# Issuing the 32 loads of weight halves from SP in place of ACT in a fused attention and feed-forward kernel

## The chip, the cores and the metric

The kernel runs on one core of a Trainium2 chip. The metric is the device time of one execution in microseconds (us), as the median of several runs. A profile is one further execution, recorded by the hardware profiler: TensorE (PE, with its weight loads PEld), VectorE (DVE), ScalarE (ACT), GpSimd (POOL) and SyncE (SP), and the 16 DMA engines that move data between the chip's memory (HBM) and the on-chip buffers. SP and ACT both issue DMAs; such an issue is shown as SPq or ACTq.

## The reference, cut to what matters

Windowed attention with a few always visible "sink" keys, followed by a feed-forward block with a softplus between its two products:

```python
scores = scale * np.matmul(q, k.transpose(0, 1, 3, 2))      # q, k, v: 4 x 8 heads x 768 x 64
keep = is_sink | in_window                                   # 4 sinks, window of 128
a = softmax(np.where(keep, scores, -1e9))
x = (a @ v).transpose(0, 2, 1, 3).reshape(3072, 512)
h = x @ w_in                                                 # 512 x 2048
out = (np.maximum(h, 0.0) + np.log1p(np.exp(-np.abs(h)))) @ w_out
```

The two weight matrices arrive as 64-bit floats, 16.8 MB together.

## The kernel before, in words

The 3072 rows are cut into 12 chunks of 256. Each chunk goes through the attention of its 8 heads, then through 8 blocks of the feed-forward part. The program is a software pipeline over heads: while chunk n is in the feed-forward part, chunk n+1 is in attention.

The weights are read once. `_weight_dma` (line 358) loads one half block of 512 KB in raw form: `wi` is the first matrix, `wo` the second, the first digit is the block, the second the half, and an `r` at the end marks the raw words (`wi20r`). There are 32 such loads, each into a buffer of its own, so none waits for a buffer. After the load a half is turned into two 32-bit parts in four stages: a cast of the upper words into a scratch tile `upper` (stage a, on DVE, ACT or POOL), a shift-and-or into a word tile (stage c, line 403, always DVE), a rounded high part (d) and the rest (l). Stage a is the first reader of the raw words.

The first 17 head steps are written out by hand in the string `START` (letters are parts of the pipeline, numbers are heads); after that a steady loop runs. In `START` the letter `w` loads the next weight half, `L8`, `L10`, ... load the keys and queries of a pair of heads, `S7` computes the scores of head 7, `T7` its softmax, and `a c d l` take the next half through the four stages. Heads 0 to 7 belong to chunk 0, heads 8 to 15 to chunk 1. In the names of tiles the chunk comes first: `k1_2`, `q1_2` are keys and queries for heads 2 and 3 of chunk 1.

PE and SP issue their instructions in the order in which the program is written. ACT, DVE and POOL get an order that a scheduler worked out at build time. Each engine then goes through its order strictly: an instruction whose inputs are not there holds up all behind it on that engine.

Two kinds of waits matter for a DMA. First, buffers: keys of pairs from head 6 on share two buffers (`tag="qkh"`), so `k1_2` can be loaded only when PE has finished `S7`, the last reader of `k0_6`; likewise `k1_4` waits for `S9`, and `qk2_1` for `S15`. Second, semaphores: the built program gives eight completion semaphores to the DMAs of SP and ACT in turn, and a DMA is issued only after the last one that used its semaphore has landed. So about eight are in flight at a time.

Of the kernel before, what the change touches and what calls it, by code (L numbers as in the profile page):

```python
# [14 lines left out]
I16 = mybir.dt.int16  # L15
# [18 lines left out]
WH = WC // 2  # L34
# [323 lines left out]
def _weight_dma(c, s, k, half):  # L358

    src = c.a["w"][s, k, :, half * WH : (half + 1) * WH]
    tag = f"{WTAG[k]}{s}{half}"
    r = c.wp.tile([P, 4 * WH if c.w64 else 2 * WH], I16 if c.w64 else F32, tag=tag, name=f"{tag}r")
    if c.w64:
        c.nc.scalar.dma_start(r[:, : 4 * WH - 1], src.bitcast(I16)[:, 1:])
    else:
        c.nc.scalar.dma_start(r[:, :WH], src)  # L370
    c.raw[s, k, half] = r


# [136 lines left out]
def _fast(c):  # L510
# [23 lines left out]
    def dma(i):  # L534
        if dmas:
            _weight_dma(c, *dmas.pop(0))
# [135 lines left out]
def _general_weights(c):  # L672

    nc = c.nc
    for e in ((s, k, half) for s in range(FP) for k in range(2) for half in range(2)):
        _weight_dma(c, *e)
        r = c.raw[e]
        t = c.stg.tile([P, WH], I32, tag="stg", name="gt%d_%d_%d" % e)
        if c.w64:
            mid, top16 = _weight_words(r)  # L680
            top = c.gp.tile([P, WH], I32, tag="g_top", name="gtop%d_%d_%d" % e)
            u = c.gp.tile([P, WH], I32, tag="g_u", name="gu%d_%d_%d" % e)
            nc.vector.tensor_copy(top[:], top16.bitcast(I16))
            nc.vector.tensor_scalar(u[:], top[:], 4, 0x7FF, ALU.logical_shift_right, ALU.bitwise_and)
            nc.vector.tensor_scalar(u[:], u[:], -896.0, 0.0, ALU.add, ALU.max)
            nc.vector.tensor_scalar(u[:], u[:], 255.0, None, ALU.min)
            nc.vector.tensor_scalar(t[:], top[:], 19, 0x00780000, ALU.logical_shift_left, ALU.bitwise_and)
            nc.vector.scalar_tensor_tensor(t[:], u[:], 23, t[:], ALU.logical_shift_left, ALU.bitwise_or)
            nc.vector.scalar_tensor_tensor(t[:], top[:], -0x80000000, t[:], ALU.bitwise_and, ALU.bitwise_or)
            nc.vector.scalar_tensor_tensor(t[:], mid, 13, t[:], ALU.logical_shift_right, ALU.bitwise_or)  # L690
        else:
            nc.vector.tensor_copy(t[:].bitcast(F32), r[:, :WH])
        c.word[e] = t
        _weight_high(c, e, "A")
        _weight_low(c, e, "V")
# [208 lines left out]
```

## Time and profile before

| what | value |
|---|---|
| time, median of 3 runs | 738.54 us (738.09 to 738.70) |
| the profiled execution: its own time, its span | 735.03 us, 733.3 us |
| PE busy in the span | 699.0 us (95%) |
| DVE, ACT, POOL busy | 567.5 us (77%), 448.7 us (61%), 429.0 us (59%) |
| bytes moved by DMA | 63.21 MB, 16.77 MB of it on ACT's queue |
| size of a load: weight half, k, q, vr of chunk 0, qk of one head | 511.8, 200, 256, 128, 2 x 164 KB (KB of 1024 bytes) |

Shares are averages over the whole span. The page's 40 slices show that the first seventh is another stage than the rest: there DMA and DVE digits are high and PE's digits are not yet all nines; after it PE stands at 9 until the last slice. The change touches only loads that are issued in this first part, so the rows below come from there.

### The profile page before, as it was taken

The numbers are of one execution on the slowest core, as the hardware profiler recorded it, in microseconds if no ns is written. First come the engines' busy times: TensorE is split into PE (matmuls) and PEld (weight loads), VectorE is DVE, ScalarE is ACT, GpSimd is POOL, SyncE is SP. The second block draws the span as 40 slices with busy tenths as digits, with TensorE's granted clock in tenths as the row PEclk, the third lists the DMA queues.
The fourth block names the chain that finished last, engine by engine and source line by source line (L and its number), as shares of the span: only waits on it lengthen the run. The fifth ranks groups of instructions, "written<-read, shape, count | busy, mean of one in ns | idle before, by whom it ended". The sixth has DMA issues, their size and how long they took to land.

```text
span 733.3 us, 13867 instructions
## 1 busy us (share of the span) xinstructions
PE 699.0 (95%) x4489; PEld 621.4 (85%) x4489; DVE 567.5 (77%) x1608; ACT 448.7 (61%) x1098; POOL 429.0 (59%) x773
## 2 busy tenths in 40 slices
PE   4788899999999999999999999999999999999996
PEld 3567688988999999888898999998898998998995
DVE  5899997887887887887987988888887887754331
ACT  3577865765666666765666765765666666644331
POOL 4866476675655765775765665666666576563110
PEclk9899999999999999999999999999999999999998
DMA  8877611411321321312222222221222222100001
GB/s 299 298 261 227 196 40 48 119 53 44 100 67 48 106 67 49 103 55 60 74 74 67 77 77 67 77 75 46 71 66 78 77 67 77 60 11 1 29 1 35
DMA packets 40876, 63.21 MB, mean 86 GB/s; under 512 B 4635, under 2 KB 22363, under 8 KB 40795
## 3 DMA queue, kind: packets, MB, share of 16 engines
q1 hardware_dynamic: 36042, 45.47, 21.4%
q10 hardware_dynamic: 4752, 16.77, 6.7%
q8 instruction: 38, 0.62, 0.4%
q14 instruction: 44, 0.35, 0.2%
HBM read 55.93 MB, written 6.29 MB: 85 GB/s over the span
## 4 chain that ended last, share of the span: by engine, by line
PE 80%; DVE 7%; ACT 5%; POOL 5%; issue 2%; DMA 1%; ACTq 0%; SPq 0%; POOLq 0%; DVEq 0%
PE h L459 33%; PE acc L496 10%; PE acc L498 10%; PE acc L497 10%; PE x L333 6%; PE t L297 2%; PE s L230 2%; PE s L231 2%; ACT a L250 2%; PE x L327 2%; PE s L227 1%; DVE wt L403 1%; ACT mt L467 1%; ACT mt L468 1%; POOL vs L159 1%
## 5 line engine op out<-in xcount | busy, mean ns | idle before, releaser
L459 PE MATMUL h<-xh,wi 128*128 128x256 f32 x1536 | 254.1, 288 | 0.0
L459 PEld LDWEIGHTS h<-xh,wi 128*128 128x128 f32 x1536 | 211.7, 192 | 1.3 <-issue 0.3
L52 POOL TENSOR_SCALAR gh<-mt 128x512 fp32r<-128x512 f32 x91 | 56.6, 622 | 169.4 <-DVE mt L474 164.3
L459 PE MATMUL h<-xl,wi 128*128 128x256 f32 x768 | 154.7, 283 | 0.0
L496 PE MATMUL acc<-wo,gh 128*128 128x512 f32 x384 | 152.3, 397 | 0.0
L498 PE MATMUL acc<-wo,gl 128*128 128x512 f32 x384 | 151.3, 394 | 0.8 <-DVE gl L56 0.8
L497 PE MATMUL acc<-wo,gh 128*128 128x512 f32 x384 | 151.1, 393 | 0.0
L474 DVE SCALAR_TENSOR_TENSOR mt<-h,mt 128x512 f32<-128x512 f32 x96 | 66.1, 689 | 73.0 <-ACT mt L468 63.9
L466 ACT ACTIVATE mt<-h 128x512 f32<-128x512 f32 x96 | 57.1, 595 | 102.6 <-PE h L459 102.1
L459 PEld LDWEIGHTS h<-xl,wi 128*128 128x128 f32 x768 | 119.8, 192 | 0.0
L250 ACT ACTIVATE a<-a,stats 128x136 f32<-128x136 f32 x192 | 76.1, 397 | 59.7 <-DVE stats L249 59.7
L264 POOL TENSOR_SCALAR a<-a,rc 128x128 f32<-128x128 f32 x180 | 68.1, 390 | 43.0 <-ACT mt L466 28.3
L498 PEld LDWEIGHTS acc<-wo,gl 128*128 128x128 f32 x384 | 72.4, 189 | 17.7 <-DVE gl L56 1.2
L496 PEld LDWEIGHTS acc<-wo,gh 128*128 128x128 f32 x384 | 72.4, 189 | 13.0 <-issue 0.5
L56 DVE TENSOR_TENSOR gl<-mt,gh 128x512 fp32r<-128x512 f32 x96 | 77.4, 806 | 4.1 <-POOL gh L52 4.0
L497 PEld LDWEIGHTS acc<-wo,gh 128*128 128x128 f32 x384 | 72.5, 189 | 8.9
L308 POOL TENSOR_SCALAR_AFFINE_SELECT pt<-tl 128x256 fp32r<-128x256 f32 x80 | 57.9, 724 | 17.6 <-DVE tl L56 17.6
L467 ACT ACTIVATE mt<-mt 128x512 f32<-128x512 f32 x96 | 60.8, 633 | 3.1
L468 ACT ACTIVATE mt<-mt 128x512 f32<-128x512 f32 x96 | 60.7, 632 | 3.1
L48 ACT CAST qkh<-qk 128x656 fp32r<-128x656 f32 x80 | 59.5, 744 | 2.4 <-DMA qk<-qk 2.3
L308 POOL TENSOR_SCALAR_AFFINE_SELECT pt<-th 128x256 fp32r<-128x256 f32 (+1 forms) x96 | 41.8, 435 | 27.5 <-ACT th L48 20.2
L56 DVE TENSOR_TENSOR kl<-qk,qkh 128x400 fp32r<-128x400 f32 x80 | 53.7, 671 | 2.5
(183 smaller groups left out, 1247.2 us busy)
## 6 DMA issues: line engine op xcount, KB each, us to landing
qk<-qk SPq DMA_DIRECT2D x160, 164.0 KB, 3.0
vr<-v SPq DMA_DIRECT2D x32, 192.0 KB, 2.8
out<-o SPq DMA_DIRECT2D x24, 256.0 KB, 2.3
q<-q SPq DMA_DIRECT2D x8, 256.0 KB, 4.9
vr<-v SPq DMA_DIRECT2D x16, 128.0 KB, 2.2
k<-k SPq DMA_DIRECT2D x8, 200.0 KB, 4.8
wi00r<-w ACTq DMA_DIRECT2D x1, 511.8 KB
wi01r<-w ACTq DMA_DIRECT2D x1, 511.8 KB
```

The lines of the kernel that those rows point to most:

```text
L48: nc.scalar.copy(out, in_)
L56: (nc.vector if eng == "V" else nc.gpsimd).tensor_tensor(out, a, b, ALU.subtract)
L250: nc.scalar.activation(a, a, AF.Exp, bias=nm, scale=-1.0, accum_out=sm[:, j : j + 1])
L264: (nc.vector if eng == "V" else nc.gpsimd).tensor_scalar(a, a, rc[:, j : j + 1], 0.0, ALU.mult, ALU.add)
L308: nc.gpsimd.affine_select(pt[:, e, :, 1], src[:], [[0, CH], [1, P]], ALU.is_ge, 0.0, base=0, channel_multiplier=-1)
L459: nc.tensor.matmul(h[:, j], wt, x, start=k == 0, stop=k >= len(prods) - 2, skip_group_check=True)
L467: nc.scalar.activation(t[:], t[:], AF.Exp, scale=-1.0)
L468: nc.scalar.activation(t[:], t[:], AF.Ln, bias=1.0)
L474: nc.vector.scalar_tensor_tensor(t[:], h[:], 0.0, t[:], ALU.max, ALU.add)
L496: nc.tensor.matmul(acc[:], gh[:, j, q], wh, start=f == 0, stop=False, skip_group_check=True)
L497: nc.tensor.matmul(acc[:], gh[:, j, q], wl, start=False, stop=False, skip_group_check=True)
L498: nc.tensor.matmul(acc[:], gl[:, j, q], wh, start=False, stop=f == 2 * FP - 1, skip_group_check=True)
```

## The change

`_weight_dma` is called by the letter `w` of `START` and, in the fallback path, by `_general_weights`. Its DMA is now issued by SP (`nc.sync`) where it was issued by ACT (`nc.scalar`). Nothing else is edited; the fallback path isn't entered with these inputs.

```diff
@@ _weight_dma
     if c.w64:
-        c.nc.scalar.dma_start(r[:, : 4 * WH - 1], src.bitcast(I16)[:, 1:])
+        c.nc.sync.dma_start(r[:, : 4 * WH - 1], src.bitcast(I16)[:, 1:])
     else:
-        c.nc.scalar.dma_start(r[:, :WH], src)
+        c.nc.sync.dma_start(r[:, :WH], src)
```

SP before, the stretch between the last loads of chunk 0 and those of chunk 1 (`k1_0`: chunk 1, heads 0 and 1; the last number of a name is only a count):

```order
L201 DMA vr0_2_176<-v 128x2x128
L174 DMA k1_0_210<-k0 128x400
L176 DMA q1_0_212<-q0 128x512
L174 DMA k1_2_249<-k0 128x400
L176 DMA q1_2_251<-q0 128x512
L201 DMA vr0_3_391<-v 128x2x128
L174 DMA k1_4_485<-k0 128x400
```

SP now, from the same `k1_0` on:

```order
L174 DMA k1_0_210<-k0 128x400
L176 DMA q1_0_212<-q0 128x512
L368 DMA wi11r_214<-w 128x2047
L368 DMA wo00r_216<-w 128x2047
L174 DMA k1_2_249<-k0 128x400
L176 DMA q1_2_251<-q0 128x512
L368 DMA wo01r_253<-w 128x2047
L368 DMA wi20r_275<-w 128x2047
L368 DMA wi21r_312<-w 128x2047
L368 DMA wo10r_314<-w 128x2047
L368 DMA wo11r_334<-w 128x2047
L368 DMA wi30r_367<-w 128x2047
```

Six weight loads now stand behind `k1_2`, which waits for `S7`. On ACT the same stretch, as a difference (minus is before, plus would be now):

```order
 L250 ACTIVATE a_0_178,sm_2_234<-a_0_178,stats 128x136 x2
 L48 COPY th_0_244<-t_0_241 128x256
-L368 DMA wo01r<-w 128x2047
 L250 ACTIVATE a_0_178,sm_3_263<-a_0_178,stats 128x136 x2
 L262 ACTIVATE a_0_178<-a_0_178,rc_0_179 128x128 x2
-L368 DMA wi20r<-w 128x2047
 L250 ACTIVATE a_1_277,sm_4_279<-a_1_277,stats 128x136 x2
 L48 CAST upper_167<-wi01r 128x512
```

ACT loses its issues and keeps the order of the rest. The orders of DVE, POOL and PE in this path are the same in both programs.

## Rows read from the trace of the kernel before

**Rows 1.** Stages: busy us of each engine (instructions), PE clock, DMA share, GB/s

```profile
20.00:40.00 20.00, 15.89 (x75) 10.19 (x73) 18.85 (x67) 10.86 (x40) 17.04 (x26) 0.95 0.87 286
...
80.00:100.00 20.00, 17.72 (x118) 14.87 (x118) 19.64 (x48) 13.98 (x32) 8.20 (x14) 1.00 0.39 98
100.00:120.00 20.00, 20.00 (x125) 16.94 (x123) 16.03 (x43) 11.84 (x29) 14.04 (x25) 1.00 0.16 45
80.00:85.00 5.00, 3.47 (x29) 3.24 (x29) 4.93 (x10) 4.02 (x9) 2.32 (x4) 1.00 0.88 209
```

**Rows 2.** Chain that ended last, 8 to 50 us: start, us, engine, tile, line

```profile
12.68 0.09 ACTq L368
...
29.79 0.47 DVE upper L50
30.25 0.38 DVE s L243 x2
...
48.03 0.09 ACTq L368
```

**Rows 3.** Timeline of SP's issues, 24 to 33 us: start, us, line, out<-in

```profile
24.95 0.33 SPq L174 DMA_DIRECT2D k<-k  x1
25.32 0.60 SPq L176 DMA_DIRECT2D q<-q  x1
25.96 0.43 SPq L201 DMA_DIRECT2D vr<-v  x1
32.15 0.33 SPq L174 DMA_DIRECT2D k<-k  x1
```

**Rows 4.** Timeline of PE, scores of pairs of heads: S7, S9, S12

```profile
23.86 1.06 PE L227 MATMUL s<-k,q 128*128 128x264 f32 x4
...
30.99 1.13 PE L227 MATMUL s<-k,q 128*128 128x264 f32 x4 [1.11 <-DVE stats L249]
...
45.38 1.05 PE L227 MATMUL s<-k,q 128*128 128x264 f32 x4
```

**Rows 5.** Timeline of ACT's issues: two weight halves

```profile
12.44 0.33 ACTq L368 DMA_DIRECT2D wo01r<-w  x1
16.35 0.33 ACTq L368 DMA_DIRECT2D wi20r<-w  x1
```

**Rows 6.** Timeline of DVE, 28.9 to 34 us: start, us, line, out<-in

```profile
28.96 0.16 DVE L256 TENSOR_SCALAR sm<-sm 128x2 f32<-128x2 f32 x1
...
29.24 0.44 DVE L50 CAST upper<-wo01r 128x512 f16<-128x512 bf16 x1
...
29.70 0.55 DVE L50 CAST upper<-wi20r 128x512 f16<-128x512 bf16 x1
...
30.98 0.73 DVE L403 SCALAR_TENSOR_TENSOR wt<-wo01r,upper 128x512 int32<-128x512 int32 x1
...
32.40 0.98 DVE L256 TENSOR_SCALAR sm<-sm 128x2 f32<-128x2 f32 x1
...
33.49 1.71 DVE L403 SCALAR_TENSOR_TENSOR wt<-wi20r,upper 128x512 int32<-128x512 int32 x1
```

**Rows 7.** DMA issues: engine, count, KB each, us from issue to landing

```profile
wi30r<-w ACTq DMA_DIRECT2D x1, 511.8 KB, 6.3
...
wi51r<-w ACTq DMA_DIRECT2D x1, 511.8 KB, 5.1
...
wo50r<-w ACTq DMA_DIRECT2D x1, 511.8 KB, 10.2
```

**Rows 8.** Timeline, 75 to 84 us: the load of qk2_1, the cast of wi70

```profile
75.06 1.11 SPq L181 DMA_DIRECT2D qk<-qk  x2
...
83.07 0.77 ACT L48 CAST upper<-wi70r 128x512 f16<-128x512 bf16 x1
```

**Rows 9.** Timeline of POOL, 32 to 35 us: low parts of weight halves

```profile
32.09 1.26 POOL L56 TENSOR_TENSOR wi<-wt,wi 128x512 fp32r<-128x512 f32 x1
33.39 1.27 POOL L56 TENSOR_TENSOR wo<-wt,wo 128x512 fp32r<-128x512 f32 x1
```

## The prediction, made before the changed kernel had run

> **What bounds the kernel now.** I read the busy shares first, then stages of 20 us, then the chain of waits in the stage where the loads lie, then the timelines of SP, PE and DVE there, and last the list of DMA issues. Over the whole span PE is the busiest engine, and in the stage from 100 to 120 us it is busy all 20.00 us [rows 1]. But the 32 loads are issued before that, and there another engine sets the pace: DVE is busy 18.85 us of 20 in the stage from 20 us and 19.64 us in the one from 80 us, the first and the last of four such stages, while PE has 15.89 and 17.72 [rows 1]. The reader is to see in the chain that around 30 us it runs on DVE from one instruction to the next: the cast of a weight half into `upper`, then the softmax of scores [rows 2]. So a stop of DVE at 30 us has no cover: what stands behind it feeds ACT, POOL and PE, and PE is full after 100 us and has no room to win time back. DMA engines are busy 0.87 of the stage from 20 us and move 286 GB/s, so a full stretch carries 286 / 0.87 = 329 GB/s, or 321 KB per us [rows 1].
>
> **The change part by part.** *ACT loses 32 issues.* One takes 0.33 us or somewhat more of ACT's sequencer [rows 5], at least 32 x 0.33 = 10.6 us in all. ACT does arithmetic for 10.86 us of 20 in the stage from 20 us [rows 1], so most of it lies beside idle time. On the chain, issues of line 368 appear as five pieces of about 0.09 us, the first at 12.68 and the last at 48.03 us [rows 2]: 5 x 0.09 = 0.45 us to gain. The bounds are 0 (ACT only waits a little longer for DVE) and 10.6 us (every issue on the path); I take 0.45, since the chain shows the pieces themselves.
>
> *SP gains the 32 issues, in the order in which the program is written.* The first five halves stand ahead of `k1_2` in SP's order. Before, SP came to `k1_2` early and stood at it: it was issued at 24.95 us [rows 3], and S7, whose four matmuls release its buffer, started at 23.86 and ended 1.06 us later, at 24.92 [rows 4]. The wait has been harmless, because only loads of keys, queries and values stood behind it. Now six weight halves stand there. Of these ACT issued `wo01` at 12.44 and `wi20` at 16.35 us [rows 5], some 13 and 10 us ahead of the point at which SP can pass S7. Nothing in the change moves S7: its inputs are loaded before the first half, and up to 24 us DVE, POOL and ACT read only halves that stay ahead of the wait.
>
> *When the two halves come.* SP issues `k1_2` at 24.95, `q1_2` at 25.32, and the third load, now `wo01`, at 25.96; the one after that follows 0.43 us later [rows 3], so `wi20` at 26.4 us. The nearest row for its landing is `wi30`, which before was issued beside the same `k1_2` and `q1_2` and took 6.3 us [rows 7]: `wi20` lands at 26.4 + 6.3 = 32.7 us. Before, DVE cast `wo01` at 29.24 and `wi20` at 29.70 us [rows 6]. DVE will stop at the first and again at the second, and the second ends it: 32.7 - 29.70 = 3.0 us late. From below: the four loads are 200 + 256 + 512 + 512 = 1480 KB, 4.6 us at the full rate, which from 24.95 ends at 29.6 us if issue and landing cost nothing at all, that is no stop. The shortest landing of a half, 5.1 us [rows 7], gives 31.5 us and a stop of 1.8 us. From above: the longest landing, 10.2 us in a deep queue [rows 7], gives 36.6 and 6.9 us. I take 3.0: the queue behind k and q is that of `wi30`.
>
> *What stands behind the stop.* On DVE the softmax of the next head, whose end released PE for S9 in the chain; S9 began at 30.99 us after a wait of 1.11 us for DVE [rows 4]. S9 in turn releases `k1_4`, issued at 32.15 us [rows 3], so the next gate on SP moves with DVE. Then the DMA queue is full and the consumers have moved 3 us back as well. The tightest of the following loads is `q1_4`, read by S12 at 45.38 us [rows 4]. From `k1_2` to `q1_4` the new order has 200 + 256 KB, six halves, 128 KB of `vr0_3`, three halves, and 200 + 256 KB: 456 + 3072 + 128 + 1536 + 456 = 5648 KB, 17.6 us at 321 KB per us. With 6.3 - 4.6 = 1.7 us for issue and landing, it is there at 24.95 + 1.7 + 17.6 = 44.3 us; S12 will ask at about 45.38 + 2.6 = 48.0 us. It costs nothing, with 3.7 us of cover.
>
> *The last halves.* `wi70` to `wo71` now stand behind `qk2_1`, which waits for S15: 75.06 us before [rows 8], 77.6 now. SP issues two transfers and then `wi70`, about 78.8; with 6.3 us it lands at 85.1, and ACT casts it at 83.07 + 2.6 = 85.7 us [rows 8]. This is covered by 0.6 us, and the later halves are read later still.
>
> *Sum.* +3.0 - 0.45 = +2.55 us on the profiled execution: 735.03 + 2.55 = 737.6 us. Its span is 733.3 us, and the 1.7 us around it do not change. The median of the runs, 738.54 us, stands 3.5 us above the profiled execution; the same addition gives 741.1 us.
>
> **A rule that speaks against this.** The stage from 20 us shows the 16 DMA engines 0.87 busy whichever of the two engines issues [rows 1], and the change moves no byte more. The Trainium skill, "DMA: Bandwidth & Descriptors", section "Issuing engines are not separate DMA queues", says that DMAs from different issuers share the same 16 engines and that issuing from several only saves the sequencer's issue time, usually small beside the transfer. By that rule alone the sum would be the 0.45 us on ACT and no more; it becomes rival A. The trace agrees that an issue is short, 0.33 us [rows 5], but it also shows SP standing at a buffer's wait until 24.95 us [rows 3], which the rule does not speak of.
>
> **The rivals.** *A, the place of the issue does not matter.* The halves come in time after all, because SP's gate opens earlier or the data of the first 25 us runs ahead. For it: half the loads before the gate are in the same order as before. Against it: even at the full rate without any latency the second half would be there at 29.6 us, a tenth of a microsecond before its use. Time: 738.54 - 0.45 = 738.1 us.
>
> *B, the stop is paid back on DVE.* Not slower: in 32 to 35 us POOL works on low parts of halves, 1.26 and 1.27 us [rows 9], and DVE's rows beside them are long: `sm` takes 0.98 us where one at 28.96 took 0.16, the shift-and-or 1.71 where the one before took 0.73 [rows 6]. If DVE's stop lets POOL get through before DVE reaches these, 0.82 + 0.98 = 1.8 us return. It decides when the stop is no longer than these 1.8 us, the shorter of the bounds above: 738.54 + 1.8 - 1.8 - 0.45 = 738.1 us. Against it: POOL's second row works on a half that ACT rounds behind DVE's softmax, so it moves with DVE and meets it again.
>
> *C, a second stop at S12.* The slowest busy stretch, from 80 to 85 us, carried 209 GB/s at 0.88, 238 GB/s or 232 KB per us [rows 1]. At that rate `q1_4` is there at 24.95 + 1.7 + 24.3 = 51.0 us, 3.0 after S12 asks: 744.1 us. For it: one queue now holds the keys behind nine halves. Against it: the stage in question has run at 329.
>
> *D, faster.* ACT's issues cost more than the chain shows, since a wait for a semaphore stops ACT too. If a third of the 10.6 us lay on the path and the halves came in time, 738.54 - 3.5 = 735.0 us. Against it: DVE, not ACT, is full in these stages [rows 1].
>
> **How the numbers follow.** A measurement of this kernel can tell about 0.2% from no change, 1.5 us. The forecast, one stop of DVE for about 3 us, has 0.52, with 739.8 to 742.6 us as its own range; 0.03 of it lies within 1.5 us. A has 0.15, B 0.08, C 0.13, D 0.12. Slower is 0.52 - 0.03 + 0.13 = 0.62, the same 0.15 + 0.08 + 0.03 = 0.26, faster 0.12. The range leaves out most of D and the top of C and of the upper bound: 737.8 to 744.3 us.
>
> **What would show it.** Right: SP's `k1_2` still issued near 25 us with the weight halves right behind; idle time on DVE before the casts of `wo01` and `wi20` near 30 us, put down to their DMAs, 3 us together; a dip of the DMA rate between 20 and 26 us; PE's later work the same and shifted by 2 to 3 us. Wrong: no wait on DVE for a weight half (A), DVE's `sm` and shift-and-or near 33 us short (B), PE waiting for q at S12 (C), or ACT's chain shorter by microseconds (D). The forecast fails altogether if S7 ends much earlier than 24.9 us, or if the loads before the gate are slower in one queue than in two, so that a half ahead of it comes late.

## The result, and the profile after

The changed kernel takes 740.87 us (median of 6 runs, 739.32 to 742.90), the kernel before, run beside it, 738.12 us (6 runs): a ratio of 1.0048, 95% interval 1.0032 to 1.0065, so 2.4 to 4.8 us slower. The profiled execution took 739.32 us with a span of 737.6 us, 4.3 us more than that of before; the rows below explain these two executions, while the medians lie 2.75 us apart. The engines' busy times changed little (PE 699.5 us, DVE 564.5, ACT 448.7, POOL 427.8; DVE has 3.0 us less than before), so the time lies in waits.

SP first: the timeline of its issues from 25 to 36 us (start, us, engine queue, line, operation, tile), to be laid beside [rows 3].

```profile
25.56 0.33 SPq L174 DMA_DIRECT2D k<-k  x1
25.94 0.43 SPq L176 DMA_DIRECT2D q<-q  x1
26.41 0.43 SPq L368 DMA_DIRECT2D wo01r<-w  x1
26.89 0.43 SPq L368 DMA_DIRECT2D wi20r<-w  x1
...
29.85 1.01 SPq L368 DMA_DIRECT2D wi30r<-w  x1
30.90 0.62 SPq L201 DMA_DIRECT2D vr<-v  x1
31.56 0.52 SPq L368 DMA_DIRECT2D wi31r<-w  x1
33.72 0.33 SPq L368 DMA_DIRECT2D wo20r<-w  x1
35.22 0.33 SPq L368 DMA_DIRECT2D wo21r<-w  x1
```

`k1_2` is still let through by S7, 0.6 us later than before, and the six halves follow at once. The timeline of DVE from 29.7 us shows what that does; the bracket at a row's end is the idle time before it and what ended it. It answers to [rows 6].

```profile
29.76 0.17 DVE L257 RECIPROCAL rc<-sm 128x2 f32<-128x2 f32 x1
33.73 0.46 DVE L50 CAST upper<-wo01r 128x512 f16<-128x512 bf16 x1 [3.80 <-DMA wo01r<-w]
34.08 0.21 DVE L269 TENSOR_TENSOR sa<-a,rc 128x64 f32<-128x64 f32 x1
35.23 0.46 DVE L50 CAST upper<-wi20r 128x512 f16<-128x512 bf16 x1 [0.94 <-DMA wi20r<-w]
...
37.83 0.16 DVE L256 TENSOR_SCALAR sm<-sm 128x2 f32<-128x2 f32 x1
38.02 0.17 DVE L257 RECIPROCAL rc<-sm 128x2 f32<-128x2 f32 x1
38.10 0.67 DVE L403 SCALAR_TENSOR_TENSOR wt<-wi20r,upper 128x512 int32<-128x512 int32 x1
...
41.85 0.74 DVE L243 COPY_PREDICATED s<-diag,s 128x128 f32<-128x128 int32 x2 [1.90 <-PE s L227]
```

DVE stands for 3.80 us before the cast of `wo01` and for 0.94 us before that of `wi20`: 4.74 us in all, where before it had no wait for a weight half. `wo01` comes into use 33.73 - 26.41 = 7.3 us after its issue and `wi20` 8.3 us. The second is now a link of the chain that ended last (start, us, what), where before the chain around 30 us went from one DVE instruction to the next [rows 2]:

```profile
26.89 8.32 DMA wi20r<-w
```

The SP rows tell the same from another side. Eight loads can be in flight, so the eleventh from `k1_2` on, `wo20`, waits for the third to land: it goes out at 33.72, as DVE's cast of `wo01` begins. The twelfth goes out at 35.22, as the cast of `wi20` begins.

The same stretches as windows (start:end; length, then busy us and count of PE, PEld, DVE, ACT and POOL; granted PE clock; DMA share; GB/s), to be read against [rows 1]:

```profile
20.00:26.00 6.00, 5.75 (x26) 3.72 (x25) 5.16 (x19) 3.02 (x13) 4.51 (x6) 0.76 0.00 0
26.00:32.00 6.00, 3.83 (x18) 2.44 (x18) 3.64 (x16) 2.52 (x9) 5.78 (x13) 1.00 0.73 219
32.00:34.00 2.00, 0.00 (x0) 0.00 (x0) 0.27 (x1) 0.00 (x0) 1.03 (x1) 0.79 1.02 334
34.00:36.00 2.00, 0.00 (x0) 0.00 (x0) 1.06 (x6) 0.00 (x0) 0.00 (x0) 0.50 0.95 328
36.00:40.00 4.00, 3.08 (x8) 1.83 (x9) 3.52 (x17) 2.03 (x7) 0.01 (x1) 0.50 1.03 406
```

From 20 to 26 us the DMA engines now move nothing; before they moved 291 GB/s there. The next 6 us run at 219 GB/s. The clock column falls to 0.50, the lower of the two levels (1.2 GHz), after PE has had no work from 30.5 us on. PE's timeline shows the price at S9, the row that answers to the middle one of [rows 4], and then S10, the scores of the next head:

```profile
24.48 1.06 PE L227 MATMUL s<-k,q 128*128 128x264 f32 x4
...
36.42 2.10 PE L227 MATMUL s<-k,q 128*128 128x264 f32 x4 [5.92 <-DVE stats L249]
...
41.20 1.06 PE L227 MATMUL s<-k,q 128*128 128x264 f32 x4
```

S9 starts after 5.92 us of waiting for DVE (1.11 before) and takes 2.10 us in place of 1.13. S10 follows on PE without a further wait for DVE, and DVE waits 1.90 us for S10 (its row at 41.85 above). In the kernel before it was PE that waited there; S10 on PE and its first reader on DVE:

```profile
35.87 1.16 PE L227 MATMUL s<-k,q 128*128 128x264 f32 x4 [1.36 <-DVE stats L249]
```

```profile
36.62 0.29 DVE L243 COPY_PREDICATED s<-diag,s 128x128 f32<-128x128 int32 x1 [0.20 <-PE s L227]
37.07 0.29 DVE L243 COPY_PREDICATED s<-diag,s 128x128 f32<-128x128 int32 x1 [0.15 <-PE s L227]
```

From 63 us on the shift is carried unchanged. SP's transfers of keys for a later chunk, released by PE's work, come at 98.65 us where they came at 94.46: 4.19 us late, and the span is 4.3 us longer. Nothing is won back after 100 us. The late gate is seen in SP's timeline and, as a second piece, in ACT's [rows 8]:

```profile
79.17 1.10 SPq L181 DMA_DIRECT2D qk<-qk  x2
80.32 0.58 SPq L368 DMA_DIRECT2D wi70r<-w  x1
```

```profile
87.23 0.78 ACT L48 CAST upper<-wi70r 128x512 f16<-128x512 bf16 x1
```

`wi70` is issued at 80.32 us and cast 6.9 us later without a wait.

### The profile page after: what moved, and what is told of

The parts are those of the page before. It is cut to its first block, busy times and chain, and to the rows that moved or that the text cites. A ratio compares the mean times of both kernels' runs of the same rounds, so it can differ in the third digit from the quotient of the medians.

```text
span 737.6 us, 13865 instructions
## 1 busy us (share of the span) xinstructions
PE 699.5 (95%) x4489; PEld 621.5 (84%) x4489; DVE 564.5 (77%) x1608; ACT 448.7 (61%) x1098; POOL 427.8 (58%) x773
## 4 chain that ended last, share of the span: by engine, by line
PE 80%; DVE 6%; ACT 5%; POOL 5%; DMA 2%; issue 1%; SPq 0%; POOLq 0%; ACTq 0%; DVEq 0%
PE h L459 33%; PE acc L496 10%; PE acc L498 10%; PE acc L497 10%; PE x L333 6%; PE t L297 2%; PE s L230 2%; PE s L231 2%; PE x L327 2%; PE s L227 2%; ACT a L250 1%; DMA wi20r<-w 1%; POOL pt L308 1%; POOL vs L159 1%; ACT mt L467 1%
```

## The experiments

The question was whether the 0.48% come from the late halves at all, and if so what makes them late: the gate, SP as the issuer, or what is ahead of them in the queue. In all twelve kernels PE, DVE, POOL and ACT keep the order of their arithmetic; only issues of loads move. Each was compared with new runs of the kernel before on the same chip.

**Only two halves given back to ACT (e1), and only two on SP (e2).** The edit, shortened:

```diff
+    eng = c.nc.scalar if (s, k, half) in ((0, 1, 1), (2, 0, 0)) else c.nc.sync   # e1: wo01, wi20
+    # e2: the same with "not in"
-        c.nc.sync.dma_start(r[:, : 4 * WH - 1], src.bitcast(I16)[:, 1:])
+        eng.dma_start(r[:, : 4 * WH - 1], src.bitcast(I16)[:, 1:])
```

> As the changed kernel, but wo01 and wi20 alone are issued by ACT again; 30 halves stay on SP. Theory G (gate): the change is slower because SP stands at k1_2 until S7 and these two halves behind it come late for DVE. Then DVE has no wait for a half near 30 us and the time is that of before within 1.5 us, 736.5 to 739.5. Rival Q (one queue): the loss comes from all loads sharing SP's queue, whatever stands at the gate. Then two loads out of 32 change little and it stays 2 to 4 us above before. Rival L (the later halves): wi21 to wi30 or wi70 to wo71, which still stand behind the gates, cost part of it; then it lies 1 to 2 us above before.

> The opposite half: only wo01 and wi20 are issued by SP, behind k1_2; the other 30 halves stay on ACT. Theory G: DVE still stops for them, 3 to 6 us, and the time lies 2 to 5 us above before, about that of the changed kernel. Rival Q: with 30 of 32 loads on ACT's queue the time is that of before within 1.5 us.

Measured: e1 735.70 us against 736.78, ratio 0.9990 (0.9978 to 1.0002), no wait of DVE for a half. e2 743.56 us, ratio 1.0067 (1.0041 to 1.0093), with waits of 3.7 us for `wo01` and 1.8 us for `wi20`. So 30 of the 32 loads may be issued by SP for nothing, and the two that stand closest behind the gate cost about as much alone as all 32 do (more by the ratio, but the intervals overlap). In e2's profile the gate came later still, at 26.98 us, and behind its stop of 5.5 us DVE waited another 4.0 us for PE.

**The gate put behind the halves (e3), and both gates (e6).**

```diff
# e3, START: k1_2 and q1_2 are loaded behind six halves
-... W0 L10 w N2 S4 ... a S7 c O1 ...
+... W0 w N2 S4 ... a S7 L10 c O1 ...
# e6 has besides, for qk2_1
-... W11 a L17 c V10 ... D1 a S15 E1 ...
+... W11 a c V10 ... D1 a S15 L17 E1 ...
```

> All 32 halves on SP as in the changed kernel, but the load of k1_2 and q1_2 stands in SP's order after the six halves, at the place where S7 ends anyway. Orders of PE, DVE, ACT and POOL are those of the changed kernel. Theory G: the six halves go out before 20 us, DVE has no wait for a half near 30 us, time as before or up to 1 us less (ACT's issues gone): 737 to 738.5. Rival Q: one queue is as crowded as in the changed kernel, 740 to 742.

> All 32 halves on SP; the loads that wait for a buffer are moved in SP's order to where their buffer comes free anyway: k1_2 behind the six halves, and qk2_1 behind wi70 to wo70. The prediction said that the second gate costs nothing because it is covered: then the time is that of the kernel with k1_2 alone moved, 736.4, within 1 us. Rival: the last halves did cost something there; then it is 1 to 2 us faster than that kernel.

Measured: e3 736.39 us against 736.78, ratio 0.9991 (0.9978 to 1.0004), span 733.1 us, the halves issued between 11.66 and 16.69 us, no wait for them. e6 735.50 us against 737.15, ratio 0.9983 (0.9970 to 0.9997). With all 32 loads on SP, moving the one gated pair `k1_2` and `q1_2` removes the whole loss; the issuer as such costs nothing that these runs resolve. For the second gate, e6 lies 0.6 us below e3 by the ratios, which these runs do not resolve either. e6 has the lowest median of the versions tried.

**The kernel before with late halves on ACT (e4).**

```diff
# START of the kernel before: six tokens w moved from ahead of S7 to behind it
-... d w a S7 c O1 ...
+... d a S7 w w w w w w c O1 ...
```

> The kernel before, all 32 halves on ACT, but the six halves wo01 to wi30 are issued by ACT only near 24 us, about when S7 ends. Theory G, which says that lateness alone counts and not the issuer: DVE stops for wo01 and wi20 by 2 to 5 us and the time lies 2 to 5 us above before. Rival Q: two queues as before, so the time of before within 1.5 us.

Measured: 741.29 us against 736.78, ratio 1.0058 (1.0041 to 1.0076). The time is what lateness would give, but not by lateness: DVE did not wait for any half. ACT's timeline shows why.

```profile
26.97 0.60 ACTq L368 DMA_DIRECT2D wo11r<-w  x1
31.39 0.33 ACTq L368 DMA_DIRECT2D wi30r<-w  x1
31.77 0.37 ACT L48 CAST xh<-x 128x256 fp32r<-128x256 f32 x1 [5.81 <-DMA k<-k]
```

`wi30` was the ninth load in flight, and ACT stood at its issue until `k1_2` had landed, with a cast behind it that DVE (6.4 us) and PE waited for. The run says nothing on lateness alone. It shows rival D's mechanism, which neither the kernel before nor the changed one has.

**Fewer loads ahead of or behind the two (e5, e7, e8).**

```diff
# e5: behind k1_2 and q1_2 only wo01, wi20 and vr0_3; the other halves behind k1_4
-... S5 c W1 w w d ... d V1 w c ... T6 d w a S7 ... W4 w T8 c V3 S9 O3 w w K4 ... L12 w O4 ...
+... S5 c W1 d ... d V1 c ... T6 d a S7 ... W4 T8 c V3 S9 O3 K4 ... L12 w w w w w w w w O4 ...
# e7: wo01 ahead of the gate, wi20 behind it
-... W0 L10 w N2 ...
+... W0 w L10 N2 ...
# e8: load split in two; q1_2 (letter M) behind wo01 and wi20
-... a w T4 ...
+... a w M10 T4 ...
```

> As the changed kernel, but behind k1_2 and q1_2 only wo01, wi20 and vr0_3 follow; the four next halves and three more stand behind k1_4, which waits for S9. Question: why did wo01 and wi20 take 7.3 and 8.3 us from issue to use and not 6.3. Theory D (depth): because six more loads stood in the queue and shared the DMA engines. Then they land in 6.5 us or less, DVE stops 3 us in all, and the time is 1 to 2 us below the changed kernel. Rival R (restart): the queue moves slowly for some 6 us after the gate whatever follows, since the changed kernel carried only 216, 189 and 252 GB/s in the three 2 us after 26 us. Then the stop stays 4.5 to 5 us and the time is that of the changed kernel, about 3.5 above before.

> As the changed kernel, but wo01 is issued ahead of k1_2; only wi20 of the two that DVE needs first stands behind the gate. Theory G with a stop that reaches the end one to one: wi20 lands 1.6 to 2.4 us earlier than in the changed kernel (512 KB less ahead of it), DVE stops once, 2.5 to 3.2 us, and the time lies 1.5 to 2.5 us above before, between the two kernels. Rival: the loss comes from DVE's wait for wo01, 3.8 of the 4.7 us in the changed kernel; with it gone only 0.9 us of stop are left and the time is that of before.

> As the changed kernel, but q1_2 (256 KB) is issued behind wo01 and wi20. Theory R with bytes: at the 216 GB/s that the changed kernel carried just after the gate 256 KB are 1.2 us, so both halves land about 1.2 us earlier and the time falls by about 1 us against the changed kernel. Rival F: what is slow after the gate is a fixed start of the queue and not what stands ahead; then the stop stays within 0.3 us of 4.7.

Measured:

| | time, before (us) | ratio (95%) | gate | `wo01`: issue to use, DVE's wait | `wi20`: issue to use, DVE's wait |
|---|---|---|---|---|---|
| e5 | 743.11, 737.15 | 1.0079 (1.0055 to 1.0103) | 27.01 | 5.2, 1.6 | at most 6.3, none |
| e7 | 739.96, 737.15 | 1.0037 (1.0022 to 1.0052) | 27.59 | ahead of the gate | 6.2, 2.2 |
| e8 | 739.18, 737.15 | 1.0039 (1.0025 to 1.0053) | 25.25 | 4.8, 0.8 | 6.6, 1.5 |

Each takes 1.7 to 2.5 us off the 7.3 and 8.3 us of the changed kernel, so what is in flight beside a half bears on its landing. As times e5 is a miss: its stop shrank to 1.6 us, but DVE then waited 2.7 us for PE, and ACT 2.2 us for `wi21`, one of the halves that had been put off. In e8 the stop was 2.3 us and DVE waited another 4.0 us for PE, whose clock was at the lower level from about 33 to 43 us; in e7 it was 2.2 us and again 4.0 us, with the clock at 0.50 from 36 to 44 us. So in e5, e7 and e8 the wait for PE is longer than the stop itself.

**Late halves on ACT without the blocked cast (e9, e10).**

```diff
# e9, against e4: five w behind S7, the sixth two steps later
-... a S7 w w w w w w c O1 ... a T7 c V2 ...
+... a S7 w w w w w c O1 ... a T7 c w V2 ...
# e10, against e9: the five one step later
-... a S7 w w w w w c O1 W3 ...
+... a S7 c O1 w w w w w W3 ...
```

> The kernel before (ACT issues all halves), with the tokens of wo01, wi20, wi21, wo10, wo11 moved behind S7 and that of wi30 behind ACT's next cast xh and the next softmax row. In e4 ACT stood 5.8 us at the issue of wi30, the ninth load in flight, until k1_2 had landed, with the cast xh behind it, so that run said nothing on lateness alone; here xh stands ahead of that issue. The theory that the lateness of wo01 and wi20 is what costs, whichever engine issues them: DVE casts wo01 and wi20 only after waits for their DMAs, 3 to 6 us together, S9 late by as much, median 1.003 to 1.008 of the kernel before. The rival that the issue on SP is what costs (SP's queue, its order or its rate): no DVE wait for a half, or under 1 us, and the median within 0.2% of the kernel before. If ACT again stands microseconds at an issue with arithmetic behind it that DVE waits for, the run tells neither.

> As e9 (ACT issues the halves, SP the keys and queries), but the tokens of wo01, wi20, wi21, wo10 and wo11 stand one step later, behind ACT's cast xh, in the 1.9 us in which ACT waits for DVE in the kernel before. So no arithmetic that is due stands behind them, and they are issued from about 25.5 us, under 1 us earlier than in the changed kernel, but from another engine than k1_2 and q1_2 beside them. Two queues faster than one (e9 moved 340 GB/s in 26 to 32 us, the changed kernel 219): wo01 and wi20 land within 6.7 us, by 32.7, DVE stops 2 to 3 us in all, median 1.001 to 1.004 of the kernel before. Lateness alone, whatever the queue: landing after 7.3 to 8.3 us, a stop of 4 to 5 us, median 1.004 to 1.007.

Measured: e9 737.57 us against 736.51, ratio 1.0014 (1.0003 to 1.0025), no wait for a half, and 2.0 us of DVE waiting for ACT, whose cast came 1.5 us late behind five issues. e10 737.85 us against 737.19, ratio 1.0008 (0.9994 to 1.0022). e10 issues both halves within 0.1 us of when the changed kernel does. ACT's issues and DVE's casts in its timelines:

```profile
26.48 0.33 ACTq L368 DMA_DIRECT2D wo01r<-w  x1
26.84 0.46 ACTq L368 DMA_DIRECT2D wi20r<-w  x1
```

```profile
31.43 0.44 DVE L50 CAST upper<-wo01r 128x512 f16<-128x512 bf16 x1
32.20 0.58 DVE L50 CAST upper<-wi20r 128x512 f16<-128x512 bf16 x1 [0.24 <-DMA wi20r<-w]
```

They are used 5.0 and 5.4 us after issue, in place of 7.3 and 8.3, and DVE waits 0.24 us. Halves issued at 26.4 us need not land as late as in the changed kernel; this fell against the plain theory of lateness, and by more than the expectation for two queues allowed. Part of the missing stop is no merit of the loads, though: in e10's profile S7 ended only at 27.12 us, and DVE reached the cast of `wo01` at 31.43, where in the changed kernel it stood ready from 29.93. With e10's landing times the changed kernel would still have stopped for up to about 2 us (an estimate: 26.41 + 4.95 - 29.93 = 1.4 for `wo01`, and some 0.4 for `wi20`). And `k1_2` was issued at 27.15 us in e10, behind the two halves in time as well as in another queue, so two causes were left.

**One queue, two orders (e11, e12).** Here ACT issues `k1_2` and `q1_2` too, so that one queue carries all; e11 has them ahead of the halves, as the changed kernel does, e12 behind `wo01` and `wi20`.

```diff
# both, in load, for k1_2 and q1_2
-                nc.sync.dma_start(k[:], c.a["k0"][chunk, h // 2])
+                eng = nc.scalar if (chunk, h) == (1, 2) else nc.sync
+                eng.dma_start(k[:], c.a["k0"][chunk, h // 2])      # and q[:] alike
# START
-... a S7 c O1 w w w w w W3 ...
+... a S7 c O1 L10 w w w w w W3 ...      # e11
+... a S7 c O1 w w L10 w w w W3 ...      # e12
```

> As e10, but ACT issues k1_2 and q1_2 too, right ahead of wo01 (behind xh, when S7 is done, so without a wait at the gate): the order and the times of issue of the changed kernel, in one queue again, and that of ACT. If what slows the halves is one queue with k and q ahead of them: about 220 GB/s in 26 to 32 us, DVE stops 4 to 5 us for wo01 and wi20, median 1.004 to 1.008 of the kernel before, over 0.2% slower than e10. If it is SP's own queue: over 300 GB/s, a stop under 3 us, and the time of e10.

> As e11 (k1_2, q1_2 and the halves all issued by ACT, one queue), but wo01 and wi20 are issued ahead of k1_2 and q1_2; nothing else moves. In e10 wo01 and wi20 were in another queue than k and q and also issued ahead of them, and were used without a wait 5.0 and 5.4 us after issue; in e11 they were behind them in one queue and DVE waited 1.6 us, wo01 landing 6.2 us after issue. If it is what is ahead of them in the queue: wo01 and wi20 used within 5.5 us of issue, DVE waits under 0.7 us for them, median 0.999 to 1.003 of the kernel before. If it is that one queue carries everything: landing after 6 to 7 us, DVE waits 1 to 2.5 us, median 1.003 to 1.006.

Measured: e11 739.82 us against 737.19, ratio 1.0045 (1.0027 to 1.0062); e12 736.86 us against 737.49, ratio 0.9994 (0.9980 to 1.0008). e11, ACT's queue and then DVE:

```profile
25.20 0.33 ACTq L175 DMA_DIRECT2D k<-k  x1
...
25.58 0.45 ACTq L177 DMA_DIRECT2D q<-q  x1
26.05 0.45 ACTq L369 DMA_DIRECT2D wo01r<-w  x1
26.54 0.44 ACTq L369 DMA_DIRECT2D wi20r<-w  x1
```

```profile
32.23 0.47 DVE L50 CAST upper<-wo01r 128x512 f16<-128x512 bf16 x1 [1.59 <-DMA wo01r<-w]
...
33.80 0.44 DVE L50 CAST upper<-wi20r 128x512 f16<-128x512 bf16 x1
...
40.87 0.74 DVE L244 COPY_PREDICATED s<-diag,s 128x128 f32<-128x128 int32 x2 [2.36 <-PE s L228]
```

and e12, the same two views:

```profile
24.83 0.33 ACTq L369 DMA_DIRECT2D wo01r<-w  x1
25.20 0.45 ACTq L369 DMA_DIRECT2D wi20r<-w  x1
...
25.75 0.39 ACTq L175 DMA_DIRECT2D k<-k  x1
26.18 0.44 ACTq L177 DMA_DIRECT2D q<-q  x1
```

```profile
30.42 0.44 DVE L50 CAST upper<-wo01r 128x512 f16<-128x512 bf16 x1
...
30.87 0.55 DVE L50 CAST upper<-wi20r 128x512 f16<-128x512 bf16 x1
```

e11 has the cost of the change although ACT issues all 32 halves, and exchanging two pairs of loads takes all of it away. Ahead in the queue, the halves go out 1.2 to 1.3 us sooner and are used at most 5.6 and 5.7 us after issue; behind `k1_2` and `q1_2`, `wo01` needs 6.2 and `wi20` landed after 7.0 us by the list of issues. DVE was ready for `wo01` 4.6 us after its issue in e11 and 5.6 us after in e12, so of e11's stop of 1.6 us 1.0 is the later issue, and at least 0.6 the longer landing. In 26 to 32 us e12 moves 330 GB/s and e11 271. The windows also show what the stop does to PE's clock; first e11, then e12:

```profile
32.00:34.00 2.00, 0.00 (x0) 0.00 (x0) 1.77 (x3) 0.00 (x0) 1.79 (x3) 0.66 1.01 315
34.00:36.00 2.00, 1.03 (x3) 0.85 (x4) 1.65 (x8) 1.14 (x5) 0.00 (x0) 0.50 0.98 362
```

```profile
32.00:34.00 2.00, 1.35 (x6) 0.87 (x6) 1.60 (x7) 1.55 (x7) 1.97 (x3) 1.00 1.03 387
34.00:36.00 2.00, 1.99 (x10) 1.43 (x11) 1.97 (x9) 0.71 (x2) 1.35 (x1) 1.00 1.02 416
```

e11's stop for the halves is only 1.6 us, yet PE, which waited 4.85 us for DVE before S9 (1.74 in e12), falls to 0.50 and DVE waits 2.4 us for S10. That second wait is the larger part there. The clock shows it over all runs, and not only in the profiled ones: its mean over the span was 0.981 to 0.988 in the runs of the changed kernel, e2, e5, e7, e8 and e11, which stop for a half, and 0.986 to 0.994 in those of e1, e3, e6, e10 and e12, which do not or hardly do.

What the expectations missed besides: e11's stop (4 to 5 us expected, 1.6 measured), whose time came out as expected because of the wait for PE; and the times of e2 and e7, 6.8 and 2.8 us above before by the medians where at most 5 and 2.5 were expected, with the same wait for PE in them.

## Why the prediction was right, and where not

**The mechanism and the time: right.** 741.1 us was forecast, 740.87 measured. SP's `k1_2` stays near 25 us with the halves right behind, DVE stops at exactly the two casts named, the transfers dip to nothing from 20 to 26 us, and PE's later work is shifted. e1, e2 and e3 show that these two halves and their place behind the gate carry the cost. How close the time came is in part luck: the same addition put the profiled execution at 737.6 us, and it took 739.32. The median stood 3.5 us above the profiled execution before, and only 1.6 us above it now.

**The stop was mis-sized: 3.0 us forecast, 4.74 measured** (inside the bounds of 1.8 and 6.9). The term that failed is the landing time: 6.3 us taken for `wi20`, 8.3 measured. The step was "I take 3.0: the queue behind k and q is that of `wi30`". But before, `wi30` went out on ACT's queue at 24.26 us, ahead of `k1_2` at 24.95, so its 6.3 us [rows 7] were never those of a load behind k and q. The prediction looked at which loads were neighbours, not at which was first. In e11, behind k and q, the two halves needed 6.2 and 7.0 us, in e12, ahead of them, at most 5.6 and 5.7. The order is not all of it: in e5 they stood behind the same k and q, but with only `vr0_3` behind them, and needed 5.2 and at most 6.3 us. S7 ended at 25.54 in place of 24.92 us, and the gate came later with it; but DVE came to its cast 0.6 us later as well, so this adds to the time and not to the stop. The Trainium skill, "DMA: Bandwidth & Descriptors", section "Two DMAs through the same engine are not ordered", says that descriptors within one queue of a DMA engine start in order, though pipelined; e11 and e12 agree with it.

**Rival B's payback was real, 1.86 us.** `sm` took 0.16 us and the shift-and-or of `wi20` 0.67, where they had taken 0.98 and 1.71 [rows 6]: 0.82 + 1.04. The argument against it (POOL's second row moves with DVE and meets it again) fails: POOL's 34 to 36 us window is empty, its next row only starts at 39.99 us after an idle time of 6.97. But B does not hold as a case, since the stop is not paid back on balance.

**A cost that no step had.** The payback was nearly used up by DVE's wait of 1.90 us for S10. From the start of S9 to that of S10 PE needed 36.42 to 41.20, 4.8 us, with no wait for DVE; before it was 4.9 us, 1.4 of them such a wait, so 3.5 us of its own. The 1.3 us more lie at the lower clock, 1.0 of them in S9 itself. Of the 4.3 us: 0.6 (S7) + 4.7 (stop) - 1.9 (B) + 1.6 (the wait for S10, 1.90 in place of 0.35) = 5.0, and DVE's rows from 46 to 59 us do run 5.0 us later than before; smaller terms in between cancel. The rest is won back by 63 us, where three waits that DVE had before (0.24 and 0.15 us for PE at 56 us, 0.46 for ACT at 58) are gone: from there on its rows run 4.2 us later. So the forecast's closeness owes something to terms that cancel.

**ACT's 0.45 us.** By its ratio e3 is 0.7 us faster than before with an interval from 1.6 faster to 0.3 slower: it agrees with 0.45, and with no gain at all.

**Rival A, the issuer does not matter,** is refuted for this order and true for others. The rule that stood behind it (the Trainium skill, "DMA: Bandwidth & Descriptors", section "Issuing engines are not separate DMA queues") holds where the halves do not stand behind a wait: e1, e3 and e12 lie within 0.1% of before, with 30 or 32 loads on SP or all on ACT.

**Rivals C and D.** C, a second stop at S12, did not come: S12 began at 50.60 us, and PE waited for no DMA from 40 to 60 us. D, 3.5 us faster, is bounded by e3 and e6, which have no issue of a half on ACT and no stop: their intervals end at 1.6 and 2.2 us faster than before. The last halves were forecast as covered, and were: `wi70` used 6.9 us after its issue without a wait; both times about 1.5 us later than forecast, as the larger shift says.

**What stays open.** S7 ended between 24.2 (e6) and 27.6 us (e7) in kernels that had the same work ahead of it. The traces show where the time went, in PE's own speed. The eight score matmuls from about 10.1 us, in the changed kernel and in e7:

```profile
10.12 2.02 PE L227 MATMUL s<-k,q 128*128 128x264 f32 x8 [0.65 <-PE s L227]
```

```profile
10.17 3.86 PE L227 MATMUL s<-k,q 128*128 128x264 f32 x8 [0.65 <-PE s L227]
```

They take 3.8 to 3.9 us in e2, e5, e7 and e10 and 2.0 in the others, although the clock column reads 1.00 there in both. Later the granted clock comes back from 0.50 to 1.00 at about 20 us in e6, 22 before, 23 in the changed kernel and 24 to 25 in those four. Why it differs is open, and since a profile is one execution, the gate of another execution of the same kernel can lie elsewhere.

Open too is what sets the landing of a half. Behind k and q it took 7.3 and 8.3 us in the changed kernel, 7.2 and 9.0 in e2, 6.2 and 7.0 in e11, and 5.2 and at most 6.3 in e5; neither the order nor what is in flight beside it explains all of these alone.

## What to carry to other kernels

When loads move to another issuing engine, list what each of them now stands behind there: first an instruction that waits for a buffer, then the transfers that are issued just ahead. If a late gate is in the way, move the gated load behind those that are free to go, as e3 does; here that was worth more than the choice of the engine. And price a stop of one engine with what it does to the clock of the engine that waits for it.

## What the runs showed of the hardware that had not been expected

- Two 512 KB loads behind transfers of 200 and 256 KB in one queue, with four more halves right behind, landed or were used 6.2 to 8.3 us after issue (changed kernel, e11); ahead of the two, or in another queue, 5.0 to 5.7 us after (e12, e10); behind them, but with only 128 KB following, 5.2 and at most 6.3 us after (e5).
- After 6 us without a transfer the changed kernel moved only 219 GB/s in the next 6 us (DMA share 0.73), with up to eight loads in flight from 28 us on, and 406 GB/s from 36 to 40 us. The pause alone does not explain it: after such a pause (0 to 6 GB/s from 20 to 26 us) the next 6 us brought 271 GB/s in e11, 292 in e8 and 330 in e12.
- A DVE stop cost twice: with a stop of 4.74 us (changed kernel) or 1.6 us (e11) PE waited 5.92 and 4.85 us, the granted clock was 0.50 in the window from 34 to 36 us, S9 took 2.10 us in place of 1.13, and DVE then waited 1.9 and 2.4 us for PE; without a stop (e12, and 0.24 us in e10) the clock was 1.00 there.
- A DMA issue on ACT that had to wait stopped the arithmetic behind it: 5.81 us in e4, put down by the profile to the landing of `k1_2`.
